# Attention with mixed heads and two MLPs: first two pulls on two queues, two score pairs behind the first mix, weight passes four steps behind each load

## The chip, the cores and the metric

The kernel runs on one core of one Trainium2 chip. The metric is the device time of one execution in microseconds (us), lower is better. The core has five engines with an instruction queue each: PE (matrix multiplies into PSUM), ACT, DVE and POOL (elementwise work), and SP, which here only issues DMA transfers. An engine executes its queue in order; a transfer that is issued runs beside the engines.

## What is computed

The reference, cut to what matters (`B, H, S, D = 2, 12, 448, 64`):

```python
scores = scale * (q @ k^T)                       # per batch and head, 448 x 448
scores = einsum('bhij,hg->bgij', scores, w_pre)  # mix over the 12 heads
attn   = softmax(scores, axis=-1)
attn   = einsum('bhij,hg->bgij', attn, w_post)   # mix over the heads again
x      = attn @ v                                # then (B*S, H*D) = (896, 768)
h      = x @ w_in;  x = (h * relu6(h + 3) / 6) @ w_out       # 768 -> 2048 -> 768
h      = x @ w_in2; x = (max(h,0) + alpha*min(h,0)) @ w_out2 # 768 -> 2048 -> 768
```

## The kernel before

**Tiles, groups, steps.** The 896 query rows are cut into 8 tiles of at most 120 rows (120, 120, 120, 88 per batch). The scores of a tile lie in SBUF as `S[row, head, key]`; three such buffers are used in turn. Six *score pairs* make one tile: a pair is the `q k^T` of two heads (`qk_parts`, line 205, PE), brought from PSUM to SBUF by one copy on ACT and one on DVE. For the mix over heads, ten rows of all 12 heads have to lie on 120 partitions; a *pull* (`pull`, line 221) is the DMA that moves one such group of rows there, SBUF to SBUF. There are 90 groups, and a *step* `p_` treats two of them, so there are 45 steps (`NP`). The pulls of step `p_ + 3` are issued in step `p_`, into four buffers that are used in turn.

**One step.** `premix` (line 234) multiplies the two pulled groups with `w_pre`, gives the row maxima (`nm`, line 242, DVE) and lets one score pair of a later tile run between its matmuls; `exp` (line 251, ACT) gives `e` and the row sums; `norm` (lines 258 to 263) scales `w_post` by the inverse sums into `wr` (on POOL up to step 36, on DVE from step 37, `late_from`); `post` (line 274, PE) of the step before multiplies `e` with `wr`; `post_evac` (line 289) copies the result to `MT`, two copies on ACT, from the end of the score pairs on one of them on DVE. `av` (lines 320 and 341, PE) multiplies finished tiles with `v`. The scheduler is off (`tc.manual_schedule()`): every engine's order is the order in which the loop `for p_ in range(-2, NP + 1)` writes its instructions.

**Score pairs.** The table `qk_at` says in which step a pair runs. Before step 0 there are two steps, -2 and -1, that hold only pairs of tile 1, three in each; from step 0 to step 35 there is one pair in each step. The loads of `q` (`load_q_at`) hang on this table.

**Loads on SP.** All pulls and nearly all loads are issued by SP, in the order of the code: first `q` and `k` of batch 0, `w_pre`, then the pulls of steps 0 to 2 with `w_post` between the fourth and the fifth. In steps 3 to 6 `v` of batch 0 is loaded, `q` of tiles 3 and 4 in steps 3 and 6, `k` of batch 1 in steps 7 to 12, one load a step, behind the pulls of that step.

**First weight blocks.** The MLP weights come as 64-bit words and are turned into a high and a low 32-bit part by passes: `conv_abs` (line 411) and `conv_low` (417) on ACT, `conv_shift` (427, 428) and `conv_sign` (435) on DVE, `conv_round` (442) on POOL, then `conv_hi` (447, ACT) and `lo_parts` (455, POOL). Blocks 0 to 2 are loaded during the attention, each in two halves, through one staging buffer (`early_wst`), so the load of a block follows `conv_round` of the one before. The table says in which step the load begins (17, 24, 31) and when the passes run: `conv_abs` and `conv_shift` in step 19, 27, 33, `conv_low` and `conv_sign` two steps later, `conv_round` three. `conv_hi` runs in steps 38, 42 and 44. From step 38 on, ACT and POOL also split `xT` into two parts (lines 524 and 525), and from step 42 the first matmuls of the MLP (line 529) run between the steps.

Of the kernel before, what the change touches and what calls it, by code (L numbers as in the profile page):

```python
# [17 lines left out]
Q = 64  # L18
# [17 lines left out]
def kernel(  # L36
# [15 lines left out]
    nc = tc.nc  # L52
    _, D, H, S = k.shape
# [10 lines left out]
    GH = G2 * H  # L64
# [44 lines left out]
    with tc.manual_schedule():  # L109
# [26 lines left out]
        def load_q(ti, *at, qs=(nc.sync, nc.sync)):  # L136
            T = tiles[ti]
            n = T["n"]
            m = H // 2 * n
            if ti == 2:  # L140
                t = late.tile([128, WC, 2], F32, tag="early_wst", bufs=1, name="qst")
                t = q_st[ti] = t.rearrange("p n o -> p (n o)")[:, :Z + H // 2 * GP]
            else:
                t = q_st[ti] = kq.tile([128, Z + H // 2 * GP], F32, tag="qst", bufs=2, name="qst")
            nc.gpsimd.memset(t[:, :Z], 0.0)
            z = Q + m - n + upper(n)
            if z > Z + m:
                nc.gpsimd.memset(t[:, Z + m:z], 0.0)
            at = (0, *at, H // 2)
            for x, y in zip(at, at[1:]):  # L150
                for o in range(2):
                    d = slice(D * o, D * o + D)
                    a = T["i0"] * H
                    if T["b"]:
                        a += o * m
                        nc.sync.dma_start(
                            out=t[d, Z + x * n:Z + y * n], in_=q[T["b"], d, a + x * n:a + y * n]
                        )
                        continue
                    src = q[T["b"], d, a:a + H * n].rearrange("p (j o n) -> p j o n", o=2, n=n)  # L160
                    qs[o].dma_start(
                        out=t[d, Z + x * n:Z + y * n].rearrange("p (j n) -> p j n", n=n),
                        in_=src[:, x:y, o, :],
                    )
                yield
# [194 lines left out]
        qk_at, av_at, av_first = {}, {}, {}  # L360
        marked = {NTILE - 1}
        for i in range((NTILE - 1) * (H // 2)):
            p_ = i // 3 - 2 if i < H // 2 else i - H // 2
            qk_at.setdefault(p_, []).append((1 + i // (H // 2), i % (H // 2)))
        for ti in range(NTILE - 1):
            lo = (tiles[ti]["s"] + tiles[ti]["ng"] - 1) // 2 + 2
# [243 lines left out]
        for c in range(2):  # L610
            a = GH * c
            nc.sync.dma_start(out=wpre[Z + GH * c:Z + GH * c + GH, :GH], in_=w_pre[a:a + GH, a:a + GH])
        list(load_q(2))
        for _ in range(4):
            d_buf.append(late.tile([128, 2, S], F32, tag=f"pull{len(d_buf)}", bufs=1, name="pull"))
            nc.gpsimd.memset(d_buf[-1][:Z], 0.0)
# [2 lines left out]
            v_c.append(late.tile(shape, F32, tag=f"v{c}", bufs=1, name=f"v{c}"))  # L619
        seen = late.tile([128, 16], F32, tag="rest", bufs=1, name="rest")[:, :1]  # L620
        nc.gpsimd.tensor_scalar(wpre, wpre, scale, 1.0, ALU.mult, ALU.mult)

        def s_out(pairs):
            for o, (d, s_) in enumerate(pairs):
# [9 lines left out]
            also.setdefault(s_, []).extend(fs)  # L634

        before_post = {}
        for i, a in enumerate((17, 24, 31)):
            odd = (a + 2) | 1
            for z in range(2):
                at(2 * (a + z), lambda z=z, i=i: load_w(i, z, 2))  # L640
            for s_, f in ((odd, conv_abs), (odd + 2, conv_low)):
                before_post.setdefault(s_, []).append(lambda f=f, i=i: f(i))
            for s_, f in ((odd, conv_shift), (odd + 2, conv_sign), (odd + 3, conv_round)):
                at(2 * s_, lambda f=f, i=i: f(i))
# [23 lines left out]
        load_at = {}  # L668
# [4 lines left out]
                load_at.setdefault(s_, []).append(lambda b=b, x=x: load_v(b, *x))  # L673

        for c in range(H // 2):
            load_at.setdefault(7 + c, []).append(
                lambda c=c: load_k(1, c % 2, c // 2 * 2, c // 2 * 2 + 2)
            )

        for p_ in range(-2, NP + 1):  # L680
            if p_ == -2:
                for g in range(6):
                    if g == 4:
                        for c in range(2):
                            a = GH * c
                            nc.sync.dma_start(
                                out=wraw[Q * c:Q * c + GH], in_=w_post[a:a + GH, a:a + GH]
                            )
                        nc.gpsimd.tensor_copy(
                            wpost.rearrange("p (g x) -> p x g", g=H),  # L690
                            wraw.rearrange("p (x g) -> p x g", g=H),
                        )
                    pull(g)
            late_pull = None
            if 0 <= p_ < NP - 3:
                g = 2 * p_ + 6
                pull(g)
                if groups[g][0] == groups[g + 1][0]:
                    pull(g + 1)
                else:  # L700
                    late_pull = g + 1
            for f in load_at.get(p_, []):
                f()
            for ti in load_q_at.get(p_, []):
                list(load_q(ti))
            jobs = qk_at.get(p_, [])
            pair_ = None
            if 0 <= p_ < NP:
                if jobs:
                    emit, pair_ = qk_parts(*jobs[0], "sc")  # L710
                    premix(p_, emit)
                    nc.scalar.copy(*pair_[1])
                    jobs = jobs[1:]
                else:
                    premix(p_)
            two = [lambda ti=ti, j=j: qk(ti, j, "mx" if p_ < 0 and j % 2 == 0 else "sc") for ti, j in jobs]
            pend = [f() for f in (two if p_ < 0 else [])]
            if 0 <= p_ < NP:
                exp(p_)
            for s_ in pend:  # L720
                s_out(s_)
            if pair_:
                nc.vector.tensor_copy(*pair_[0])
            if p_ >= 0:
                for f in two:
                    s_out(f())
            if late_pull:
                pull(late_pull)
            for ti, a in av_first.get(p_, []):
                av(ti, a)  # L730
            kk = 2 * (p_ - (NP - KD // 2))
            if kk == 0:
                p0 = ptile()[:, :S]
            if 0 <= kk < KD:
                in_part(p0, 0, x_t, 0, kk, kk + 2)
            for f in before_post.get(p_, []):
                f()
            if 1 <= p_:
                post(p_ - 1)
                post_evac(p_ - 1)  # L740
            if 0 <= p_ < NP:
                norm(p_)
            x1_split()
            if p_ == NP:
                p1 = ptile()[:, :S]
                in_part(p1, 1, x_t, 0, 0, 2)
                gs[0, 0] = g_tile(0, 0)
                run(act1(p0, gs[0, 0], 0))
            for f in also.get(2 * p_, []) + also.get(2 * p_ + 1, []):
                f()  # L750
            for ti, a in av_at.get(p_, []):
                av(ti, a)
# [153 lines left out]
```

## Time and profile before

| | us |
|---|---|
| median of 3 runs (641.83, 645.3, 645.5) | 645.3 |
| the profiled execution, whole | 640.25 |
| its span, from the first to the last instruction | 638.5 |
| PE busy in the span | 627.0 (98%) |
| DVE, ACT, POOL busy | 415.9, 345.3, 294.0 |

The attention fills about the first 180 us of the span, the two MLPs the rest. Rows of the profile give times in us from the start of the span. In the chain of work, each piece is what the end of the program was waiting for at that time, followed back from the last instruction. In a timeline, a bracket behind a row says how long the engine sat idle before it and what ended that.

### The profile page before, as it was taken

How to read it: one execution, taken by the hardware profiler on the slowest of the kernel's cores; microseconds unless marked ns; L12 is line 12 of the kernel's file. 1: busy time of each engine (PE TensorE's matmuls, PEld its weight loads, DVE VectorE, ACT ScalarE, POOL GpSimd, SP SyncE). 2: the span in 40 equal slices, each digit the busy share in tenths (PEclk: the TensorE clock that was granted, in tenths of full speed). 3: DMA queues.
4: the chain of work that ended last, by engine and by line, in shares of the span. 5: the costliest groups of instructions: out<-in, count | busy, mean ns of one | idle time of the engine just before them, and what ended most of it. 6: DMA issues, size and time to landing. Idle time of an engine off the chain costs nothing.

```text
span 638.5 us, 15698 instructions
## 1 busy us (share of the span) xinstructions
PE 627.0 (98%) x6528; PEld 537.2 (84%) x6528; DVE 415.9 (65%) x653; ACT 345.3 (54%) x632; POOL 294.0 (46%) x241
## 2 busy tenths in 40 slices
PE   7999999999999999999999999999999999999997
PEld 3466667666799999999999999999999999999997
DVE  3765677778666878787545533599999996544301
ACT  4886888987645566655345433444444444444301
POOL 2221123324615454556774645355555556776430
PEclk9999999999999999999999999999999999999999
DMA  7677765756012323333442333123333333445202
GB/s 187 222 197 211 207 188 204 214 177 174 34 50 100 99 100 107 125 115 101 148 148 100 112 136 100 51 100 99 100 102 110 113 113 108 149 159 180 94 1 86
DMA packets 42163, 81.69 MB, mean 128 GB/s; under 512 B 19308, under 2 KB 32364, under 8 KB 42092
## 3 DMA queue, kind: packets, MB, share of 16 engines
q1 hardware_dynamic: 41516, 80.27, 39.5%
q8 instruction: 51, 0.84, 0.5%
q10 hardware_dynamic: 576, 0.41, 0.3%
q14 instruction: 20, 0.16, 0.1%
HBM read 58.65 MB, written 2.75 MB: 96 GB/s over the span
## 4 chain that ended last, share of the span: by engine, by line
PE 86%; POOL 4%; issue 4%; DMA 3%; DVE 1%; ACT 1%; POOLq 0%; SPq 0%; ACTq 0%
PE p L529 64%; PE sc L205 6%; PE pt L274 5%; PE mx L234 5%; PE av L341 4%; POOL wb L442 2%; POOL wlo L455 2%; DMA wst<-in_w_in_dram 2%; PE av L320 1%; DMA pull<-S 1%; ACT e L251 0%; DMA qst<-in_q_dram 0%; ACT wb L411 0%; DVE wb L427 0%; DVE wb L428 0%
## 5 line engine op out<-in xcount | busy, mean ns | idle before, releaser
L455 POOL TENSOR_TENSOR wlo<-wb,whi 128x768 fp32r<-128x768 f32 (+1 forms) x67 | 128.5, 1918 | 122.4 <-ACT whi L447 122.4
L442 POOL TENSOR_TENSOR wb<-wb,wst 128x768 int32<-128x768 int32 x64 | 125.6, 1963 | 81.7 <-DVE wb L435 67.5
L529 PE MATMUL p<-xh,whi 128*128 128x448 f32 x384 | 140.0, 364 | 0.0
L529 PE MATMUL p<-xl,whi 128*128 128x448 f32 x384 | 139.4, 363 | 0.0
L529 PE MATMUL p<-gl,whi 128*128 128x448 f32 x384 | 139.3, 363 | 0.0
L529 PE MATMUL p<-gh,wlo 128*128 128x448 f32 x384 | 138.9, 362 | 0.2 <-POOL wlo L455 0.2
L529 PE MATMUL p<-gh,whi 128*128 128x448 f32 x384 | 138.8, 361 | 0.0
L529 PE MATMUL p<-xh,wlo 128*128 128x448 f32 x384 | 138.3, 360 | 0.0
L427 DVE TENSOR_SCALAR wb<-wb 128x768 f32<-128x768 f32 x64 | 52.6, 822 | 83.4 <-ACT wb L411 83.4
L411 ACT ACTIVATE wb<-wst 128x768 f32<-128x768 f32 x64 | 58.0, 906 | 72.9 <-DMA wst<-in_w_out_dram 51.8
L447 ACT CAST whi<-wb 128x768 fp32r<-128x768 f32 x64 | 53.4, 834 | 47.7 <-PE p L529 29.5
L529 PEld LDWEIGHTS p<-xh,whi 128*128 128x128 f32 x384 | 72.1, 188 | 8.0 <-issue 1.6
L205 PE MATMUL sc<-kst,qst 64*64 64x448 f32 (+2 forms) x384 | 74.7, 575 | 3.7 <-DMA qst<-in_q_dram 3.7
L234 PE MATMUL mx<-pull,wpre 64*64 64x448 f32 (+2 forms) x360 | 74.6, 544 | 2.6 <-ACT e L251 1.7
L529 PEld LDWEIGHTS p<-gh,whi 128*128 128x128 f32 x384 | 72.0, 187 | 5.2
L529 PEld LDWEIGHTS p<-gh,wlo 128*128 128x128 f32 x384 | 71.9, 187 | 5.1 <-POOL wlo L455 0.6
L529 PEld LDWEIGHTS p<-gl,whi 128*128 128x128 f32 x384 | 72.1, 188 | 4.8
L529 PEld LDWEIGHTS p<-xh,wlo 128*128 128x128 f32 x384 | 71.8, 187 | 5.0
L529 PEld LDWEIGHTS p<-xl,whi 128*128 128x128 f32 x384 | 72.1, 188 | 3.9
L242 DVE TENSOR_REDUCE nm<-mx 128x1 f32<-128x448 f32 x90 | 55.1, 622 | 20.2 <-PE sc L205 8.9
L435 DVE SCALAR_TENSOR_TENSOR wb<-wst,wb 128x768 uint32<-128x768 uint32 x64 | 67.5, 1054 | 1.1
L263 POOL TENSOR_SCALAR wr<-wpost,sm 128x60 f32<-128x60 f32 x74 | 24.4, 345 | 93.8 <-DVE sm L259 46.6
(55 smaller groups left out, 772.7 us busy)
## 6 DMA issues: line engine op xcount, KB each, us to landing
wst<-in_w_out_dram SPq DMA_DIRECT2D x32, 768.0 KB
wst<-in_w_in_dram SPq DMA_DIRECT2D x27, 768.0 KB
pull<-S SPq DMA_DIRECT2D x88, 210.0 KB
wst<-in_w_in_dram SPq DMA_DIRECT2D x10, 384.0 KB
out_dram<-o SPq DMA_DIRECT2D x12, 224.0 KB
kst<-in_k_dram SPq DMA_DIRECT2D x11, 224.0 KB
qst<-in_q_dram SPq DMA_DIRECT2D x10, 180.0 KB
v<-in_v_dram SPq DMA_DIRECT2D x4, 168.0 KB
```

The source lines that it names most:

```text
L205: nc.tensor.matmul(ps[o][r:r + z - a, :S], t[D * o:D * o + D, a:z], k_[D * o:D * o + D, j, :], start=True, stop=True,)
L234: nc.tensor.matmul(ms[r][Q * c:Q * c + Q, :S], wpre[a:z], d[a:z, c, :], start=True, stop=True)
L242: nc.vector.tensor_reduce(nm, m[:, :S], axis=AX.X, op=ALU.max, negate=True)
L274: nc.tensor.matmul(ts[c][Q * z:Q * z + Q, u:u + GH], e[a:a + GH, j:j + Q], wr[a:a + GH], start=True, stop=True,)
L341: nc.tensor.matmul(by_half(p[D * o:D * o + D, a % 3, :2 * m]), v_part(T["b"], h, t), MT[ti][:, t:2 * NJ:NJ, h, :m].rearrange("p r (o x) -> ...
L411: nc.scalar.activation(t, s[:, :, 1].bitcast(F32), ACTF.Abs)
L427: nc.vector.tensor_scalar(t, t, W_MAX, W_MIN, ALU.min, ALU.max)
L435: nc.vector.scalar_tensor_tensor(u, st_t[i][:, :, 1], 0xC0000000, u, ALU.bitwise_and, ALU.bitwise_or)
L442: nc.gpsimd.tensor_tensor(n, n, st_t.pop(i)[:, :, 0].bitcast(I32), ALU.add)
L447: nc.scalar.copy(hi, b_t[i])
L455: nc.gpsimd.tensor_tensor(lo[:, a], b_t[i][:, a], w_t[i][0].bitcast(F32)[:, a], ALU.subtract)
L529: nc.tensor.matmul(p, wt[a], xt[c], start=(first and z == 0), stop=(last and z == 2))
```

## The change

Three things. First, `w_post` is loaded and laid out before any pull, and the pull of group 1 is issued by ACT's queue while SP issues the others. Second, `qk_at` is moved: two pairs each in steps -2 and -1, two in step 0 behind its mix and its `exp`, then one in each of steps 1 to 36; the loads of `q` from tile 3 on and of `k` of batch 1 move by one step with it. Third, the blocks are loaded from steps 17, 25, 33, and the passes run four steps behind: `conv_abs` and `conv_shift` in 21, 29, 37, `conv_low` and `conv_sign` in 23, 31, 39, `conv_round` in 24, 32, 40.

```diff
         for i in range((NTILE - 1) * (H // 2)):
-            p_ = i // 3 - 2 if i < H // 2 else i - H // 2
+            p_ = i // 2 - 2 if i < 4 else max(i - 5, 0)
             qk_at.setdefault(p_, []).append((1 + i // (H // 2), i % (H // 2)))
...
         list(load_q(2))
+        for c in range(2):
+            a = GH * c
+            nc.sync.dma_start(out=wraw[Q * c:Q * c + GH], in_=w_post[a:a + GH, a:a + GH])
...
         nc.gpsimd.tensor_scalar(wpre, wpre, scale, 1.0, ALU.mult, ALU.mult)
+        nc.gpsimd.tensor_copy(
+            wpost.rearrange("p (g x) -> p x g", g=H), wraw.rearrange("p (x g) -> p x g", g=H)
+        )
...
-        for i, a in enumerate((17, 24, 31)):
-            odd = (a + 2) | 1
+        for i, a in enumerate((17, 25, 33)):
+            odd = a + 4
...
-            load_at.setdefault(7 + c, []).append(
+            load_at.setdefault(8 + c, []).append(
                 lambda c=c: load_k(1, c % 2, c // 2 * 2, c // 2 * 2 + 2)
             )
...
             if p_ == -2:
                 for g in range(6):
-                    if g == 4:
-                        for c in range(2):
-                            a = GH * c
-                            nc.sync.dma_start(
-                                out=wraw[Q * c:Q * c + GH], in_=w_post[a:a + GH, a:a + GH]
-                            )
-                        nc.gpsimd.tensor_copy(
-                            wpost.rearrange("p (g x) -> p x g", g=H),
-                            wraw.rearrange("p (x g) -> p x g", g=H),
-                        )
-                    pull(g)
+                    pull(g, nc.scalar if g == 1 else nc.sync)
...
-                if jobs:
+                if jobs and p_:
                     emit, pair_ = qk_parts(*jobs[0], "sc")
                     premix(p_, emit)
```

Three places show what moves. On PE, around the first mix (`sc` is a score pair's PSUM tile, `mx` the mix's, `qst_115` is `q` of tile 1, `qst_121` of tile 2), before:

```order
L205 MATMUL sc_235<-kst_91,qst_115 64x448
L205 MATMUL sc_235<-kst_91,qst_115 60x448
L234 MATMUL mx_251<-pull_125,wpre_95 64x448 x2
L205 MATMUL sc_250<-kst_91,qst_121 64x448
L205 MATMUL sc_250<-kst_91,qst_121 60x448
L234 MATMUL mx_252<-pull_125,wpre_95 64x448 x2
L205 MATMUL sc_249<-kst_91,qst_121 64x448
L205 MATMUL sc_249<-kst_91,qst_121 60x448
L234 MATMUL mx_282<-pull_127,wpre_95 64x448 x2
```

and now:

```order
L205 MATMUL sc_221<-kst_91,qst_115 60x448
L234 MATMUL mx_232<-pull_127,wpre_95 64x448 x2
L234 MATMUL mx_233<-pull_127,wpre_95 64x448 x2
L205 MATMUL sc_247<-kst_91,qst_115 64x448
L205 MATMUL sc_247<-kst_91,qst_115 60x448
L205 MATMUL sc_248<-kst_91,qst_115 64x448
L205 MATMUL sc_248<-kst_91,qst_115 60x448
L205 MATMUL sc_255<-kst_91,qst_115 64x448
L205 MATMUL sc_255<-kst_91,qst_115 60x448
L205 MATMUL sc_256<-kst_91,qst_115 64x448
L205 MATMUL sc_256<-kst_91,qst_115 60x448
L234 MATMUL mx_274<-pull_129,wpre_95 64x448 x2
```

The first mix (`mx_232`, `mx_233`) stands in one piece ahead of the last two pairs of tile 1, and these stand ahead of the second mix; tile 2 begins one step later.

On SP, steps 6 to 8 (`v_134` and, renumbered, `v_136` are the same tile), before:

```order
L221 DMA pull<-S 120x1x448 x2
L177 DMA v_134<-in_v_dram 96x6x64
L177 DMA v_134<-in_v_dram 32x6x64
L177 DMA v_134<-in_v_dram 80x6x64
L177 DMA v_134<-in_v_dram 48x6x64
L156 DMA qst<-in_q_dram 64x720 x2
L221 DMA pull<-S 120x1x448 x2
L119 DMA kst<-in_k_dram 64x896
```

and now:

```order
L221 DMA pull<-S 120x1x448 x2
L177 DMA v_136<-in_v_dram 96x6x64
L177 DMA v_136<-in_v_dram 32x6x64
L177 DMA v_136<-in_v_dram 80x6x64
L177 DMA v_136<-in_v_dram 48x6x64
L221 DMA pull<-S 120x1x448 x2
L156 DMA qst<-in_q_dram 64x720 x2
L221 DMA pull<-S 120x1x448 x2
L119 DMA kst<-in_k_dram 64x896
```

The pulls of step 7 (used in step 10) now stand ahead of `q` of tile 4, and the pulls of step 8 ahead of the first load of `k`.

On DVE, from step 37 to the maxima of step 38, before:

```order
L289 COPY MT<-pt 128x84x5
L258 TENSOR_SCALAR sm<-sm 128x2
L259 RECIPROCAL sm<-sm 128x2
L263 TENSOR_SCALAR wr<-wpost,sm 128x60 x2
L242 TENSOR_REDUCE nm<-mx 128x1 x2
```

and now:

```order
L289 COPY MT<-pt 128x84x5
L258 TENSOR_SCALAR sm<-sm 128x2
L259 RECIPROCAL sm<-sm 128x2
L263 TENSOR_SCALAR wr<-wpost,sm 128x60 x2
L427 TENSOR_SCALAR wb<-wb 128x768
L428 TENSOR_SCALAR wb<-wb 128x768
L242 TENSOR_REDUCE nm<-mx 128x1 x2
```

The two `conv_shift` passes of block 2, which stood ahead of the maxima of step 34, now stand ahead of those of step 38; in the same way its `conv_sign` moves from ahead of step 36 to ahead of step 40.

## Rows read from the trace of the kernel before

**Rows 1.** The page, part 4: shares of the span in the chain, by engine.

```profile
PE 86%; POOL 4%; issue 4%; DMA 3%; DVE 1%; ACT 1%; POOLq 0%; SPq 0%; ACTq 0%
```

**Rows 2.** Chain in order of time (start us, length us, what), 40 to 240 us.

```profile
43.11 4.75 DMA pull<-S
47.99 1.50 PE mx L234 x3
...
50.65 0.87 PE pt L274 x49
...
94.18 0.59 PE mx L234 x2
...
95.92 1.38 PE av L341 x24
...
132.29 0.56 DVE wb L428
...
138.38 0.76 PE mx L234 x8
...
148.40 0.81 PE pt L274 x48
...
180.56 59.60 PE p L529 x297
```

**Rows 3.** Timeline of all engines (start us, length us, what), 12 to 20 us.

```profile
12.56 3.42 SPq L221 DMA_DIRECT2D pull<-S  x4
...
16.34 0.59 PE L234 MATMUL mx<-pull,wpre 64*64 64x448 f32 x2
...
18.56 0.64 ACT L251 ACTIVATE e<-mx,nm 128x448 f32<-128x448 f32 x1
...
19.34 0.59 PE L234 MATMUL mx<-pull,wpre 64*64 64x448 f32 x2 [0.51 <-ACT e L251]
```

**Rows 4.** Timeline of SP, 41 to 46 us.

```profile
41.83 1.19 SPq L156 DMA_DIRECT2D qst<-in_q_dram  x2
43.11 1.78 SPq L221 DMA_DIRECT2D pull<-S  x2
44.95 0.75 SPq L119 DMA_DIRECT2D kst<-in_k_dram  x1
```

**Rows 5.** Windows: start:end length, busy by engine, clock, DMA share, GB/s.

```profile
40.00:50.00 10.00, 8.67 (x205) 5.68 (x200) 4.74 (x12) 6.36 (x17) 1.20 (x4) 1.00 0.72 204
50.00:60.00 10.00, 10.00 (x238) 6.83 (x234) 6.70 (x16) 8.30 (x21) 1.21 (x4) 1.00 0.80 216
```

**Rows 6.** Timeline of ACT, 83 to 134 us.

```profile
83.83 0.92 ACT L411 ACTIVATE wb<-wst 128x768 f32<-128x768 f32 x1 [1.39 <-DMA wst<-in_w_in_dram]
...
86.57 0.63 ACT L251 ACTIVATE e<-mx,nm 128x448 f32<-128x448 f32 x1 [0.50 <-DVE nm L242]
...
110.16 0.91 ACT L411 ACTIVATE wb<-wst 128x768 f32<-128x768 f32 x1
...
130.66 0.92 ACT L411 ACTIVATE wb<-wst 128x768 f32<-128x768 f32 x1 [0.91 <-DMA wst<-in_w_in_dram]
...
133.48 0.63 ACT L251 ACTIVATE e<-mx,nm 128x448 f32<-128x448 f32 x1 [0.56 <-DVE nm L242]
```

**Rows 7.** Timeline of DVE, 138 to 155 us.

```profile
138.14 0.96 DVE L435 SCALAR_TENSOR_TENSOR wb<-wst,wb 128x768 uint32<-128x768 uint32 x1
...
144.81 0.41 DVE L263 TENSOR_SCALAR wr<-wpost,sm 128x60 f32<-128x60 f32 x2
...
152.78 0.60 DVE L289 COPY MT<-pt 128x420 f32<-128x420 f32 x1 [0.78 <-PE pt L274]
...
153.69 1.35 DVE L263 TENSOR_SCALAR wr<-wpost,sm 128x60 f32<-128x60 f32 x2
```

**Rows 8.** Timeline of POOL, 142 to 155 us.

```profile
142.62 1.86 POOL L442 TENSOR_TENSOR wb<-wb,wst 128x768 int32<-128x768 int32 x1
...
153.85 1.14 POOL L525 TENSOR_TENSOR xl<-xT,xh 128x448 fp32r<-128x448 f32 x1 [0.66 <-ACT xh L524]
```

## The prediction

> **What bounds the kernel now.** I read the shares of the chain first: PE holds 86% of the span [rows 1]. The chain in order of time says where: from 180.56 on it is MLP matmuls without a break for as far as I read it [rows 2], so what the attention wins or loses by then, the whole program wins or loses, and the MLP itself gives nothing. None of the edits takes work away, so only gaps in the attention's 180 us can be won. Those that the edits touch are four. At the start the second mix waits 0.51 for an `exp` [rows 3]. At 43.11 a pull stands in the chain for 4.75 us [rows 2]. And twice ACT waits for a weight block: 1.39 us before the `conv_abs` at 83.83 and 0.91 before the one at 130.66, each with a second wait for DVE behind it (0.50, 0.56); the middle block at 110.16 waits for nothing [rows 6]. Durations are those of the profiled execution, 640.25 us for a span of 638.5; the median of the runs shown is 645.3, 5 us above it, and their spread (641.83 to 645.5) is as large as all that follows. I make the sum as a difference and apply it to the median.
>
> **Start: 0 (-0.9 to +0.8).** Before, the first mix runs at 16.34 behind six pairs, its `exp` at 18.56, the second mix at 19.34 [rows 3]. Four pulls take SP 3.42 us, 0.86 each [rows 3], so a second queue brings the second pull up to 0.86 forward, and with two pairs fewer ahead of it the mix may begin that much sooner. But the gain meets a queue. The two pairs now stand behind the mix on PE and share one pair of PSUM buffers; ACT copies the first only after both halves of `exp` 0, so the second pair waits for that copy, and the second mix stands behind it on PE. `norm` 0 on DVE likewise stands behind two copies. The price of ACT's own issue is not shown for a pull; from SP's row it is 0.86, spent while it has four pairs still to copy. I take 0: the early mix buys nothing for the second one. Ends: a whole pull's issue won, or the time of one pair's copies, about one exposed `exp` pass and issue (0.64 + 0.2), lost. `w_post` before the pulls costs nothing; SP waits there for the scores anyway.
>
> The Trainium skill speaks against the two queues: "DMA: Bandwidth & Descriptors", section "Issuing engines are not separate DMA queues", says that transfers issued by different engines run on the same 16 DMA engines and only the issuing time is saved. By that rule this term can be no more than the one issue, which is the end I have; no row here shows where the two pulls would collide.
>
> **One more step with a pair: +0.9 (0 to +1.0).** Two pairs leave the stretch before the first mix, and step 36, which had none, gets one. A mix with its pair takes PE 1.74 us (94.18 to 95.92), without one 0.76 [rows 2]; the difference is 0.98. PE is the chain there, so I take nearly all of it; nothing, if PE would have waited for DVE in that step.
>
> **Pulls ahead of `q` and `k`: -1.3 (-2.7 to 0).** In step 10 the pull ends at 47.86 (43.11 + 4.75), and the mix with its pair lasts from 47.99 to 50.65, 2.66 us against 1.74: it is still waiting in the middle, for the second pull [rows 2]. SP issued `q` of tile 4 at 41.83, right ahead of these pulls at 43.11 [rows 4]; now they go first, 1.28 us sooner. The pulls of step 8 lose the `k` load ahead of them, 0.75 of issue [rows 4]. But the DMA moves 204 and 216 GB/s here at a share of 0.72 and 0.80 [rows 5], so I reckon with a backlog: a load put behind is paid for by the next pulls. What stays won at the end of the stretch is one `k` load, 64 x 896 x 4 B = 229 KB, 1.1 us at 204 GB/s. Between 1.28 and 1.1 with a little more from the `w_post` loads: -1.3. Upper end: the whole of the late mix (0.92) and its wait in full with those of the steps behind, -2.7 as an estimate; nothing, if the next mixes are late by the same.
>
> **Block 0: -1.4 (-1.9 to -0.5).** Its load keeps its step and `conv_abs` goes from step 19 to 21, about two steps later; the load had landed 1.39 into the wait, so the wait goes. The 0.50 behind it is DVE's passes standing ahead of the row maxima; it comes back in step 22, so I leave it out. The round now ends one step ahead of the next block's load, which SP must hold for it, with the pulls of step 26 behind it. They are for step 29; three steps cover it. Without that cover one round, 1.86 [rows 8], is late. Block 1 had no wait and keeps its distance: 0.
>
> **Block 2, where it was: -1.4 (-1.5 to 0).** Load from 31 to 33, `conv_abs` from 33 to 37. The 0.91 goes, and since the passes leave this place, nearly all of the 0.56 as well [rows 6].
>
> **Block 2, where it comes to: +1.5 (0 to +3.0).** Steps 37 to 40 are those in which DVE, no longer POOL, makes `wr` as well. Two `conv_shift` passes (0.56 the one [rows 2], the other taken as equal, 1.12) now stand between `wr` 37 and the maxima of step 38, and `conv_sign`, 0.96 [rows 7], ahead of those of step 40. Behind the maxima wait `exp`, `norm` and `post`; `post` at 148.40 is in the chain [rows 2]. That is 2.08 us of DVE. The widest hole behind them is the 0.78 before 152.78 [rows 7]; against it, 1.3 is exposed. Besides, `wr` takes 0.41 alone and 1.35 with POOL's split of `xT` beside it (153.85, 1.14) [rows 7, 8]; POOL's round, 1.86 [rows 8], now runs in step 40, ahead of that split, so one more `wr` may be caught: 0 to 0.94. I take 0.2 of that, together 1.5. Ends: holes take all, or 2.08 + 0.94.
>
> On this the Trainium skill is harsher: "SBUF — State Buffer", section "Who interferes with whom", says that DVE in its two-port modes and a GpSimd instruction exclude each other for a whole instruction. The 1.35 beside the 1.14 agrees with it. By that rule a `wr` that meets the start of the round would stand for all of 1.86, this term would be 1.3 + 1.86 = 3.2 and the sum 0.0; that is most of the way to the second rival below, whose price is made from rows.
>
> **Sum:** 0 + 0.9 - 1.3 - 1.4 - 1.4 + 1.5 = **-1.7 us**: 638.6 for the profiled execution, **643.6** for the median.
>
> **Rivals.**
> *The holes hold (20%).* Steps 37 to 40 hide the passes and step 36 the pair. For it: DVE has a hole of 0.78 left [rows 7], and the span's DVE is far from full. Against it: `wr` is on DVE's path there. Then -1.3 - 1.4 - 1.4 = -4.1: 641.2.
> *DVE becomes the bound at the end (17%), slower.* In steps 37 to 41 every microsecond put ahead of the row maxima comes out behind `post`, and the round catches `wr` twice: 2.08 + 2 x 0.94 = 4.0, with the pair of step 36 4.9. The gains in front are at most 1.3 + 1.4 + 1.4 = 4.1, so it ends at +0.8: 646.1. It decides from 3.2 us of DVE and POOL delay on (4.1 - 0.9). For it: the 1.35 [rows 7]. Against it: the passes may meet PE's own long steps.
> *The order of the loads does nothing (13%).* The stretch from 40 to 60 us is bound by transfer, not by order: pulls that go first make later ones late, and the new first step eats 0.3. Then -1.4 - 1.4 + 0.9 + 1.5 + 0.3 = -0.1: 645.2. For it: 216 GB/s in the second window [rows 5]; against it: the mix at 47.99 waited for pulls behind a load that is used six steps later.
>
> **How the numbers follow.** The forecast has 50%, about 642.3 to 645.1 by itself. The terms' ends, added, reach from 638 to beyond 648, but they will not all fall on one side: I take -4.5 to +1.5. The runs before lie up to 3.5 below their median, so the low end goes lower than the sum asks, and half a us for runs goes on top: 639.0 to 647.3. One per cent is 6.45 us, about what a measurement here can tell from no change. Faster by more needs every gain whole and a fast median: 6%. Slower by more needs the slower rival twice over: 3%. Within: 91%.
>
> **What would show it.** Right: no DMA wait before any of the three early `conv_abs`; the chain's pull piece at 43 gone or under 2 us; the second mix within 0.8 us of 19.34; `exp` of step 36 to that of step 37 longer by 0.9; DVE without gaps from step 37 to 40 and `post` there waiting for `wr`. Wrong: the second mix well before 18.5 (the start does give something), steps 37 to 41 no longer than before (the holes held), or a pull in the chain at a later place for as long as before. If the MLP's stretch changes its length, the ground of all this is wrong.

## The result: slower by 0.8%, and the profile after

The changed kernel takes **648.54 us** (median of 14 runs, 645.78 to 653.11), the kernel before 644.41 beside it (14 runs, 639.63 to 649.04): ratio 1.008, 95% interval 1.0051 to 1.011, that is 3.3 to 7.1 us slower. The ratio is taken over the single runs without those in a slower state, so it is not the quotient of the medians (1.0064). The prediction said 1.7 us faster and at most 647.3. The change stays within 1%, but the sign is wrong and the time lies outside the range.

The profiled execution of the changed kernel took 645.78 us, the lowest of its 14, with a span of 644.0, 5.5 more than before; the profile of before (640.25) is near the lowest of its runs too. The chain's shares, against [rows 1], show where to look:

```profile
PE 84%; POOL 4%; issue 4%; ACT 2%; DVE 2%; DMA 1%; SPq 1%; ACTq 0%; POOLq 0%; DVEq 0%
```

PE and DMA give shares up, ACT, DVE and SP gain them. Where that happens is told best by the time from one step's first `exp` to that of a later step (ACT, line 251, read off the timelines; us):

| stretch, by the starts of `exp` | before | after | block 2 alone | start alone | order alone |
|---|---|---|---|---|---|
| 0 to 2 | 5.40 | 7.77 | 5.79 | 7.77 | 5.38 |
| 2 to 7 | 13.01 | 14.65 | 13.38 | 13.47 | 13.54 |
| 7 to 9 | 7.46 | 7.42 | 6.72 | 6.80 | 7.42 |
| 9 to 13 | 16.58 | 13.43 | 17.88 | 15.66 | 13.72 |
| 13 to 20 | 25.56 | 26.07 | 26.63 | 25.61 | 25.27 |
| 20 to 27 | 22.26 | 22.49 | 22.26 | 24.01 | 22.21 |
| 27 to 34 | 24.65 | 24.14 | 23.71 | 24.70 | 26.38 |
| 34 to 37 | 9.02 | 9.70 | 9.01 | 9.70 | 10.66 |
| 37 to 44 | 24.50 | 28.98 | 28.71 | 24.64 | 24.49 |
| `exp` of step 44 at | 167.00 | 172.54 | 172.28 | 171.12 | 167.56 |

The last three columns are experiments, told below. `exp` 44 comes 5.54 us later than before, as much as the whole span grew, so the MLP behind it kept its length, as the prediction's ground wants. Three stretches lose over 1 us (0 to 2, 2 to 7, 37 to 44), one gains (9 to 13). The column of block 2 alone shows how far single executions differ: up to step 30 that kernel does the same as the one before, and yet 9 to 13 and 13 to 20 take 1.3 and 1.1 us longer.

**The start.** Timeline of the changed kernel, 12 to 23 us, against [rows 3]:

```profile
12.26 1.66 ACTq L221 DMA_DIRECT2D pull<-S  x1
...
16.20 1.10 PE L234 MATMUL mx<-pull,wpre 64*64 64x448 f32 x8
...
17.88 0.63 ACT L251 ACTIVATE e<-mx,nm 128x448 f32<-128x448 f32 x1 [1.02 <-DVE nm L242]
...
19.69 0.98 PE L205 MATMUL sc<-kst,qst 64*64 64x448 f32 x8 [1.64 <-ACT S L631]
...
20.49 0.92 PE L234 MATMUL mx<-pull,wpre 64*64 64x448 f32 x4
...
22.74 0.64 ACT L251 ACTIVATE e<-mx,nm 128x448 f32<-128x448 f32 x1
```

The first `exp` is 0.68 earlier (17.88 against 18.56). Then the second of the two pairs waits 1.64 for ACT's copy, which stands behind both halves of `exp` 0, and the second mix stands behind that pair: 20.49 against 19.34 before. `exp` 2 begins at 25.64 instead of 23.95, and the second mix, which was to stay within 0.8 of 19.34, misses that sign by 0.35.

**`q` of tile 3.** Timeline of SP and, below, the chain:

```profile
30.90 3.12 SPq L177 DMA_DIRECT2D v<-in_v_dram  x4
34.13 1.36 SPq L161 DMA_DIRECT2D qst<-in_q_dram  x2
```

```profile
34.84 3.90 DMA qst<-in_q_dram
...
38.88 1.08 PE sc L205 x8
```

It now stands in step 4, behind four loads of `v`, and lands where its first pair wants it; PE waits 1.1 us for it and steps 7 and 8 (to `exp` 7 and 8) are 2.05 us longer than their 6.79 before. Before, it was loaded in step 3, ahead of them. This profile is a mild one. Six of the runs below have the same order there. PE waited 0.85 and 1.18 us in two of them; in the other four it waited 1.70 to 2.42, its granted clock then fell to the lower of its two levels (0.50, which is 1.2 instead of 2.4 GHz), and steps 7 and 8 took 11.2 to 12.9 us. In one of the four (the run without DVE's passes; timeline, and window with the columns of [rows 5]):

```profile
40.01 1.86 PE L205 MATMUL sc<-kst,qst 64*64 64x448 f32 x8 [2.28 <-DMA qst<-in_q_dram]
```

```profile
40.00:45.00 5.00, 4.99 (x30) 2.73 (x32) 1.15 (x2) 1.88 (x5) 0.00 (x0) 0.50 0.69 190
```

**The blocks.** ACT's `conv_abs` of the three blocks waits for nothing now, against [rows 6]:

```profile
91.10 0.91 ACT L411 ACTIVATE wb<-wst 128x768 f32<-128x768 f32 x1
...
117.51 0.91 ACT L411 ACTIVATE wb<-wst 128x768 f32<-128x768 f32 x1
...
144.79 0.91 ACT L411 ACTIVATE wb<-wst 128x768 f32<-128x768 f32 x1
```

Step 20 (from `exp` 19 to `exp` 20) falls from 5.51 to 4.56, step 34 from 5.16 to 4.23.

**The end.** DVE and, below it, POOL and ACT of the changed kernel, 146 to 160 us, against [rows 7] and [rows 8]:

```profile
146.26 0.55 DVE L427 TENSOR_SCALAR wb<-wb 128x768 f32<-128x768 f32 x1
146.84 0.56 DVE L428 TENSOR_SCALAR wb<-wb 128x768 uint32<-128x768 uint32 x1
...
153.02 0.95 DVE L435 SCALAR_TENSOR_TENSOR wb<-wst,wb 128x768 uint32<-128x768 uint32 x1
...
156.44 2.66 DVE L263 TENSOR_SCALAR wr<-wpost,sm 128x60 f32<-128x60 f32 x2
```

```profile
156.14 1.81 POOL L442 TENSOR_TENSOR wb<-wb,wst 128x768 int32<-128x768 int32 x1
157.93 1.12 POOL L525 TENSOR_TENSOR xl<-xT,xh 128x448 fp32r<-128x448 f32 x1
...
148.03 0.63 ACT L251 ACTIVATE e<-mx,nm 128x448 f32<-128x448 f32 x1 [1.84 <-DVE nm L242]
...
159.73 0.64 ACT L251 ACTIVATE e<-mx,nm 128x448 f32<-128x448 f32 x1 [2.92 <-DVE nm L242]
```

`exp` 38 waits 1.84 (1.39 before) for maxima behind the two shift passes. In step 40 `wr` begins 0.30 behind POOL's round and takes 2.66 until 159.10. The row is two instructions: the first takes 1.57 and ends 0.05 behind the round (157.95), the second takes 1.17 and ends 0.05 behind the split that follows the round (159.05). `exp` 41 waits 2.92 (1.89 before). The windows there (columns as in [rows 5]) show a second price:

```profile
156.00:158.20 2.20, 0.26 (x10) 0.07 (x5) 2.13 (x4) 0.81 (x2) 2.20 (x3) 1.00 0.80 188
158.20:159.90 1.70, 1.38 (x56) 1.25 (x59) 1.70 (x3) 0.17 (x1) 0.85 (x1) 0.73 0.85 283
159.90:162.00 2.10, 2.10 (x21) 0.70 (x14) 2.03 (x8) 2.09 (x6) 0.00 (x0) 0.50 0.87 334
```

While `wr` is held, PE works 0.26 of 2.20 us; in the third window its granted clock is 0.50, with PE busy all the time. Step 43, behind it, takes 5.38 instead of 3.91.

### The profile page after: what moved, and what is told of

Read it like the earlier page. It is cut to its first block, busy times and chain, and to the rows that moved or that the text cites. A ratio compares the mean times of both kernels' runs of the same rounds, so it can differ in the third digit from the quotient of the medians.

```text
span 644.0 us, 15691 instructions
## 1 busy us (share of the span) xinstructions
PE 626.7 (97%) x6528; PEld 537.8 (84%) x6528; DVE 415.5 (65%) x652; ACT 345.2 (54%) x633; POOL 293.8 (46%) x241
## 4 chain that ended last, share of the span: by engine, by line
PE 84%; POOL 4%; issue 4%; ACT 2%; DVE 2%; DMA 1%; SPq 1%; ACTq 0%; POOLq 0%; DVEq 0%
PE p L529 64%; PE sc L205 5%; PE pt L274 5%; PE av L341 4%; PE mx L234 4%; POOL wb L442 2%; POOL wlo L455 2%; ACT e L251 1%; PE av L320 1%; DMA qst<-in_q_dram 1%; DVE nm L242 1%; ACT MT L289 1%; DVE wr L263 1%; SPq L177 0%; ACTq L221 0%
```

## The experiments

The theory at first: the loss is the slower rival's at the end, the two pairs at the start, and `q` of tile 3; the gains in front are real. The rivals to it stand in each expectation.

### 1. Block 2 back ahead of step 37, the rest as changed

```diff
-        for i, a in enumerate((17, 25, 33)):
-            odd = a + 4
+        for i, a in enumerate((17, 24, 31)):
+            odd = (21, 27, 33)[i]
```

> The changed kernel with blocks 1 and 2 as before (loads in steps 24 and 31, passes from 27 and 33); block 0 keeps its new distance. Theory A (the passes of block 2 load DVE in steps 37 to 41, where it already makes wr): exp 37 to exp 43 goes back from 24.4 us to about 20.5 (19.9 before, plus the pair of step 36), the wait of about 0.9 for block 2's load in step 34 returns, and the whole is 3 to 4 us below the changed kernel, ratio to before about 1.001. Rival B (the pair in step 36 and the order of the late steps are the cost): the stretch stays above 23 us and the whole changes by less than 1 us.

Measured: 651.32 us, ratio 1.0121 (1.0062 to 1.018) to the kernel before, so slower still. The end did what was expected: 37 to 44 took 24.27. But step 28 took 6.63 and step 34 8.73. With block 0's passes two steps later and block 1's load in the step where it was before, SP held that load for block 0's round, and step 28 waited for it; in step 34 block 2's load was late too. The chain and the windows (columns as in [rows 5]) there:

```profile
136.16 4.45 DMA wst<-in_w_in_dram
```

```profile
140.00:145.00 5.00, 2.78 (x64) 2.22 (x68) 2.86 (x6) 3.83 (x9) 0.00 (x0) 0.62 0.66 250
145.00:150.00 5.00, 5.00 (x100) 2.97 (x95) 2.73 (x9) 3.36 (x8) 0.60 (x2) 0.69 0.15 59
```

`conv_abs` waited 4.59 for block 2's second half; PE, idle for nearly half of the first window, had a granted clock of 0.69 in the second with full work. Loads and passes of successive blocks hang together through the one staging buffer: this undoes one part and breaks another.

### 2. The start: one queue, three pairs ahead, `q` of tile 3 ahead of `v`

Three single edits to the changed kernel:

```diff
-                    pull(g, nc.scalar if g == 1 else nc.sync)
+                    pull(g)
```

> The changed kernel with the pull of group 1 on SP again. In the changed kernel ACT was held 1.66 us by that issue. Theory A (the first mix waits for the pulls, and the second mix for the pairs behind exp 0, so ACT's issue costs little): first mix at 16.2 to 16.4, exp 1 at 22.4 to 22.9, as in the changed kernel (22.74). Rival B (ACT's issue is the cost at the start): exp 1 about 1.5 us earlier, near 21.2, as before (21.25).

```diff
-            p_ = i // 2 - 2 if i < 4 else max(i - 5, 0)
+            p_ = i // 3 - 2 if i < H // 2 else i - 5
```

> The changed kernel with all six pairs of tile 1 ahead of the first mix again, three in each of steps -2 and -1, none in step 0; all else as changed. Theory A (the two pairs behind exp 0 are the cost at the start): exp 0 later than 17.88, near 18.8, but exp 1 earlier, 21.2 to 21.9 instead of 22.74. Rival B (ACT's own issue of a pull is the cost): exp 1 stays at 22.7 or goes to 23 and more, since the copies of two more pairs now stand behind that issue.

```diff
-                    load_q_at.setdefault(p_ - (6 if ti == tps else 3), []).append(ti)
+                    load_q_at.setdefault(p_ - (6 if ti == tps else 4 if ti == 3 else 3), []).append(ti)
```

> The changed kernel with q of tile 3 loaded in step 3 as before, ahead of the four v loads of step 4; all else as changed. Theory A (q of tile 3 came late because it fell behind those v loads): the chain's piece of 3.90 us on that load goes, step 7 takes 2.6 instead of 4.29 us; part of it comes back in steps 9 to 11, where pulls are the limit, so exp 13 is 0 to 1 us earlier than 61.15. Rival B (the stretch is bound by transfer in any case): exp 13 does not move, and step 10 is longer by what step 7 wins.

Measured, one execution each: 649.5, 648.58 and 647.1 us; single times differ by several us from run to run, so the steps decide. With one queue `exp` 1 began at 22.73 (22.74 with two): ACT's pull, 1.66 us of issue instead of SP's 0.86 [rows 3], neither costs nor gains. With three pairs ahead `exp` 0 began at 19.30, but `exp` 1 at 21.78, which is 0.96 earlier; the change had made it 1.49 later. So the two pairs behind `exp` 0 are most of the cost. With `q` of tile 3 back in step 3, step 7 took 2.90 instead of 4.29, and 1 to 13 took 37.27 instead of 38.41: that load's place cost 1.1 us in the mild profile, and 2.8 to 4.9 against the four whose clock fell (40.11 to 42.20).

### 3. Each part alone on the kernel before

Block 2 alone:

```diff
-        for i, a in enumerate((17, 24, 31)):
-            odd = (a + 2) | 1
+        for i, a in enumerate((17, 24, 33)):
+            odd = (19, 27, 37)[i]
```

> The kernel before with one part of the change alone: block 2 loaded from step 33, its passes in steps 37 to 40. Theory A (the slower rival of the prediction: in steps 37 to 43 every microsecond of DVE's passes, and of POOL's round beside wr, comes out behind post): the stretch from exp 37 to exp 44, 24.5 us in the kernel before and 29.0 in the changed one, becomes 28 to 29.3; step 34, 5.16 in the kernel before, becomes 4.2; together +2.8 to +4.0 us, ratio 1.004 to 1.006. Theory B (the forecast's term of +1.5, most of it hidden, and something else of the change made the end longer): the stretch is 25.5 to 26.5, the whole +0.1 to +1.1 us. Theory C (the end is longer because the score pairs moved by a step): the stretch stays at 24.5 and the whole is 0.9 us shorter.

Measured: ratio 1.0027 (1.0001 to 1.0054). Step 34 fell to 4.23 and 37 to 44 took 28.71: theory A in the steps, +4.2 against -0.9. The ratio lies between A and B; its interval holds A's lower end and all of B's, so the steps decide for A and the time does not. C is out.

Start and order of loads without the blocks (the changed kernel with the table of blocks of before, so the lines of the diff above turned back):

> The changed kernel with the table of the weight blocks of before (loads from 17, 24, 31, passes in 19, 27, 33), so the new start and the new order of loads alone. Theory A: the stretch from exp 37 to exp 44 is back at 24.5 (from 29.0), the waits before the passes of blocks 0 and 2 are back (steps 20 and 34 at 5.5 and 5.2 us), the start keeps its +1.7 by step 2, steps 7 and 8 their +2.0 for q of tile 3, steps 9 to 13 their -3.6, step 37 the pair's +0.7: together +0.8 us against the kernel before, up to +2.1 if step 15 stalls again as it did in the changed kernel; ratio 1.001 to 1.003. Theory B (start and order of loads are what made the kernel slower): the ratio stays at 1.006 to 1.010.

Measured: ratio 1.0051 (1.0022 to 1.0081), between A's numbers and B's, with an interval that overlaps both; 37 to 44 is back at 24.92. So not all of the loss is at the end. With block 2 alone it makes 1.0051 x 1.0027 = 1.0078, the whole, which leaves nothing for the later passes of block 0. Step 20 took 4.28 here, though block 0 stands where it was.

The order of loads alone:

```diff
-                    load_q_at.setdefault(p_ - (6 if ti == tps else 3), []).append(ti)
+                    load_q_at.setdefault(p_ - (5 if ti == tps else 3), []).append(ti)
...
-            load_at.setdefault(7 + c, []).append(
+            load_at.setdefault(8 + c, []).append(
```

> The kernel before with only the order of loads of the change: q of tile 4 in step 7 and the loads of k in steps 8 to 13, so each behind the pulls of one more step; start, score pairs and q of tile 3 as before. Theory A (the term of -1.3 holds): the pull leaves the chain at 43, exp 7 to exp 13 falls from 24.05 to 21.9 to 22.8 us, ratio 0.997 to 0.999. Theory B (the third rival: that stretch is bound by transfer, not by order): exp 7 to exp 20 stays within 0.5 us of 49.6, ratio 0.999 to 1.002.

Measured: 643.12 us against 643.2, ratio 0.9999 (0.9969 to 1.0028), which is B's number but does not shut out A's. In its profile, against B, the pull is gone from the chain and 9 to 13 falls from 16.58 to 13.72, but step 34 takes 6.87, since `conv_abs` of block 2 waits longer than before, and then PE runs at a lower clock (timeline of ACT; window with the columns of [rows 5]):

```profile
129.71 0.89 ACT L411 ACTIVATE wb<-wst 128x768 f32<-128x768 f32 x1 [2.73 <-DMA wst<-in_w_in_dram]
```

```profile
134.00:138.00 4.00, 4.00 (x48) 1.96 (x44) 1.98 (x6) 2.78 (x8) 0.60 (x2) 0.65 0.05 19
```

The start alone (the changed kernel with the blocks of before, `k` from step 7 and `q` one step sooner, in the steps where they were):

```diff
-                    load_q_at.setdefault(p_ - (6 if ti == tps else 3), []).append(ti)
+                    load_q_at.setdefault(p_ - (7 if ti == tps else 4), []).append(ti)
...
-            load_at.setdefault(8 + c, []).append(
+            load_at.setdefault(7 + c, []).append(
```

> The kernel before with only the start of the change: w_post ahead of the pulls, the second pull on ACT's queue, two pairs behind exp 0 and one pair more in step 36; the loads of q and k in the steps in which they were, the weight blocks as before. Theory A (the two pairs in step 0 are lost time, and nothing later takes it back): exp 2 at 25.6 us instead of 23.95, step 37 at 3.3 instead of 2.6, so +2.4 us, ratio 1.0025 to 1.0045. Theory B (the steps from 7 on wait for transfers anyway, so a later start is taken back there): exp 2 at 25.6, but exp 13 within 0.5 us of 61.0; only the pair of step 37 stays, ratio 1.000 to 1.0015.

Measured: ratio 1.0073 (1.0039 to 1.0106), 2.5 to 6.8 us: by whole times the dearest part of all, above A's number with an interval that holds A's upper end. Theory A's steps are there (0 to 2 takes 7.77, step 37 3.29). `exp` 0 came at 18.75 in this profile, so `exp` 2 is at 26.51, 2.56 later than before; with the pair that is 3.2. By `exp` 13 it is 1.44, so some of it is taken back, as B says, but not kept: step 27 holds a pause in the middle of a `post` for which the chain names nothing but PE's own issue:

```profile
108.36 1.53 issue
109.89 0.50 PE pt L274 x18
```

### 4. What the passes and the round cost at the end

The changed kernel without POOL's round of block 2, then without DVE's three passes of block 2:

```diff
-                at(2 * s_, lambda f=f, i=i: f(i))
+                if (i, f) != (2, conv_round):
+                    at(2 * s_, lambda f=f, i=i: f(i))
```

> The changed kernel without POOL's conv_round of block 2 (the 32-bit add of step 40 is left out, so the high and low parts of block 2 are unrounded). Theory A (POOL's round holds DVE off for its whole length): the wr of 2.66 us beside it is 1.35 or less, and the stretch from exp 37 to exp 44 falls from 29.0 to 27.2 to 27.9 us. Theory B (the 2.66 comes from the split of xT beside it): one wr of over 2 us is still there and the stretch stays within 0.5 us of 29.0.

```diff
+                if (i, f) not in ((2, conv_shift), (2, conv_sign)):
```

> The changed kernel without DVE's passes of block 2 (conv_shift and conv_sign are left out, so block 2 is split wrongly). Theory A (every microsecond ahead of the row maxima comes out behind post): the stretch from exp 37 to exp 44 falls from 29.0 by the 2.06 us of the three passes, to 26.5 to 27.3. Theory B (holes on DVE hide half or more of them, and the round is what costs): it falls by less than 1.0 us.

Measured: without the round 37 to 44 takes 25.57, 3.4 less, twice theory A's; without the passes 27.63, 1.35 less, between A and B. The first fence is DVE without the round, the second DVE and POOL without the passes:

```profile
160.67 0.41 DVE L263 TENSOR_SCALAR wr<-wpost,sm 128x60 f32<-128x60 f32 x2
```

```profile
163.77 2.66 DVE L263 TENSOR_SCALAR wr<-wpost,sm 128x60 f32<-128x60 f32 x2
...
163.47 1.81 POOL L442 TENSOR_TENSOR wb<-wb,wst 128x768 int32<-128x768 int32 x1
```

Take the round away and `wr` in step 40 is 0.41; keep it and it is 2.66, whatever else DVE does. Without the round the stretch saves more than the 2.25 of the one `wr`, because the lower clock behind it is gone too (step 43 4.24 instead of 5.38). Without the passes steps 38 and 40 are 1.76 shorter, nearly the 2.06 that the passes take, as A says; what is missing went to step 41, which took 0.74 more with a clock that fell earlier in it.

### 5. Earlier loads instead of later passes

```diff
-        for i, a in enumerate((17, 24, 31)):
-            odd = (a + 2) | 1
+        for i, a in enumerate((16, 23, 30)):
+            odd = a + 3
```

> The kernel before, with the blocks loaded from steps 16, 23, 30 and the passes three steps behind (19, 26, 33), all else as it was: instead of later passes, earlier loads. Theory A (the waits before the passes of blocks 0 and 2 are lateness of the load alone, and the passes cost nothing where they stood): step 20 falls from 5.52 to 4.2 to 4.6 us, step 34 from 5.16 to 4.2 to 4.6, exp 37 to exp 44 stays at 24.5; -1.5 to -2.3 us, ratio 0.9965 to 0.998. Theory B (what a wait gives back is lost elsewhere, since the loads now compete with other transfers): the steps shorten but steps 15 to 18 or 27 to 33 grow by as much; ratio 0.999 to 1.002.

Measured: 640.92 us, ratio **0.9967** (0.9938 to 0.9996). Step 20 falls to 4.18, step 34 to 4.73 (a wait of 0.51 is left), and 37 to 44 stays at 24.28. The interval nearly touches 1, and step 20 alone proves little: with block 0 untouched it took 4.21 to 4.28 in three of the runs above (block 2 alone, blocks undone, start alone), where no wait for its load was left either, and 5.31 with the order alone.

The same with the order of loads of the changed kernel:

> The kernel before with the blocks loaded a step earlier (16, 23, 30, passes three steps behind) and with q of tile 4 and the loads of k one step later, behind the pulls. In the run with the order of loads alone exp 20 came 2.75 us earlier than in the kernel before, but step 34 lasted 6.87 (for block 2's load) and steps 35 and 36 at a lower clock took 1.6 more, and the median was the same. Theory A (the order's gain is real and was given back at block 2's wait): with that wait gone most of both gains stay, -3 to -5 us, ratio 0.992 to 0.996. Theory B (the stretch from 40 to 80 us is bound by transfer and its length varies from run to run; the order gives nothing): the same as with the earlier loads alone, ratio 0.9955 to 0.998.

Measured: 641.84 us, ratio 0.996 (0.9928 to 0.9991): theory B, no more than the earlier loads alone. The pulls of step 7 now go ahead of `q` of tile 4 (first fence, SP) and land in time. But those of step 8, at 45.81, stand behind it, and the second of them is in the chain (second fence) for longer than the one in [rows 2]; step 11's mix waits 0.82 for it. Against [rows 2] the wait stands one step further on. That is not shown to come from the order: with the old order and the same earlier loads a pull of step 8 is in the chain too (third fence), issued at nearly the same time:

```profile
42.45 1.69 SPq L221 DMA_DIRECT2D pull<-S  x2
44.23 1.47 SPq L156 DMA_DIRECT2D qst<-in_q_dram  x2
45.81 1.76 SPq L221 DMA_DIRECT2D pull<-S  x2
```

```profile
46.75 5.21 DMA pull<-S
```

```profile
46.78 5.23 DMA pull<-S
```

With block 2's passes four steps behind the load, but packed into steps 34 to 36:

```diff
-            odd = a + 3
+            odd = a + 3 + i // 2
...
+            t = odd + 2 - i // 2
```

(`t` is the step of `conv_low` and `conv_sign`, `t + 1` that of the round.)

> The same, with block 2's passes four steps behind its load but still ahead of step 37: conv_abs and conv_shift in step 34, conv_low and conv_sign in 35, conv_round in 36. Theory A (a wait of 0.5 us is left before conv_abs of block 2 in step 33 with the load in step 30): step 34 falls from 4.7 to 4.2, another -0.5 us against the kernel with three steps. Theory B (conv_sign right behind conv_shift stands ahead of maxima in a row and costs as much): no difference, within 0.1 per cent of it.

Measured: 643.1 us, ratio 0.999 (0.9957 to 1.0024), no better. Step 34 falls to 4.23 (5.44 in the run before this one), but steps 35 to 37 take 10.13 instead of 9.02: theory B. Its profile also has the longest pause of PE on record for which the chain names nothing else, again inside a `post`:

```profile
71.08 3.47 issue
74.55 0.36 PE pt L274 x3
```

The changed kernel with the start of before, and with it `q` of tile 3 in step 3:

> The changed kernel with the start of before (three score pairs each in steps -2 and -1, one pair in step 0 and none in step 36, all pulls on SP, w_post between the fourth and the fifth; q of tile 3 in step 3), so the later passes and the order of loads alone. Theory A (the start costs 2.4 us by the steps that it lengthens, and what was measured beyond that, 4.7 with the start alone, is scatter of the stretches behind it): 2.0 to 3.0 us under the changed kernel, ratio to the kernel before 1.003 to 1.005. Theory B (the later start costs near 5 us, since it moves all that follows against the transfers): ratio 1.000 to 1.002.

Measured: 645.06 us, ratio 1.003 (0.9996 to 1.0064): 0.5% or 3.2 us under the changed kernel (1.008), a little above A's 2.0 to 3.0, with a ratio at A's lower end; the interval is too wide to shut B out, and the 3.2 holds the place of `q` of tile 3 as well. In this profile too a pull of step 8 holds the chain, for 5.31 us.

## Why the prediction was wrong, step by step

**Block 2, where it comes to: +1.5. In the steps this term failed most; it measured +4.5** (24.50 to 28.98), and +3.0 to +4.6 in the six profiles with the passes and the round there (27.47 to 29.06), against an upper end of 3.0. What failed is the overlap. I subtracted a hole of 0.78 on DVE, but that hole is DVE waiting for `post` [rows 7], which stands behind the same maxima: it hid nothing, and the passes came out nearly whole (step 38 lost 1.12 for 1.11 us of passes, step 40 0.87 for 0.95). Step 41 lost 1.03, for which I had taken 0.2: `wr` met the round whole, 2.66 instead of 1.35. Step 43 lost 1.47 to the lower clock, which was in no term and came in three of the six. The mechanism was that of the slower rival (17%), whose chance was far too low. That its 4.0 is near the 4.5 is in part luck: the round caught `wr` in one step, not in two, and the clock made up for it. The rule that I set beside it (the Trainium skill, "SBUF — State Buffer", section "Who interferes with whom") gave 3.2 for this term, and the trace agrees with it: each of the two instructions of the 2.66 ends 0.05 behind one of POOL's, and without the round they take 0.41.

**Start: 0 (-0.9 to +0.8). It measured +1.7 in the steps to `exp` 2, and by the time of the run with it alone, the pair of step 36 included, this part missed by most** (2.5 to 6.8 us, forecast 0.9). ACT's copy does stand behind both halves of `exp` 0, as I wrote, but I priced that as one exposed pass. The pairs wait for each other through the one pair of PSUM buffers, and all of it stands ahead of the second mix: PE waited 1.64 for the copy and had one pair more, 0.98, to do. What they left empty ahead of the first mix brought it only 0.68, since PE waits there anyway (1.15 us for a copy, ahead of the last pair). The rule on issuing engines ("DMA: Bandwidth & Descriptors" of the Trainium skill, section "Issuing engines are not separate DMA queues") says that only issuing time can be saved, and the run agrees: one queue instead of two moved `exp` 1 by 0.01.

**The pair of step 36: +0.9.** Right: 3.29 instead of 2.61, +0.7.

**Pulls ahead of `q` and `k`: -1.3.** Not borne out, though not shut out either: 0.9999 alone, an interval of -2.0 to +1.8 us, and nothing seen on top of the earlier loads. 9 to 13 took 13.7 to 14.1 in three of the five profiles with the new order and `q` of tile 3 in its place, 17.3 and 17.7 in the other two, and 15.7 to 20.5 in the four with the old order; in the run with the order alone, what the stretch won was lost again by step 37. The third rival (13%) names the outcome, but its reason, that pulls which go first make later ones late, is not shown: a pull of step 8 was late with either order (5.21 and 5.31 us in the chain with the new, 5.23 with the old). And a move of the same edit was in no term: `q` of tile 3 slid behind four `v` loads, though following every load of a moved step would have found it. It is 2.05 in steps 7 and 8 of the changed kernel's profile, 1.1 by the run that turned it back, and more where the clock fell behind the wait. The order shown ahead of the prediction began at step 6, behind the place.

**Block 0: -1.4, and block 2 where it was: -1.4.** Both inside their ranges, -0.95 and -0.93, in this pair of profiles; of the wait for DVE, 0.34 is left before `exp` 20. But the waits that they remove are not steady. Block 0's was gone in three runs without any change to block 0, and block 2's, 0.91 before, was 2.73 with the order alone and absent with the start alone. So block 0's gain is not shown to be the change's.

**The sum.** With terms measured in the one profile: 1.7 + 0.7 + (2.05 - 3.61 for steps 7 to 13) - 0.95 - 0.93 + 4.48 = +3.4, of +5.5 in the profile; 1.3 more is step 15, where PE's `post` starts late, with 0.54 of issue in the chain, and the rest is small. In the median it is 648.54 - 644.41 = +4.1.

**What the runs settle, and what stays open.** The start costs 3.2 us by the steps of the run with it alone, 4.7 by that run's ratio. The clock of the runs accounts for most of the difference, as far as so few runs can tell: its four runs with a mean granted clock of 0.999 or more took 644.7 us in the mean, the 17 such runs of the kernel before beside it 641.7, so 3.0 more; but 8 of its 12 runs lay lower, against 12 of 29. Undoing the start gave 3.2 too, with `q` of tile 3 in it.

The stretch from step 9 on differs between profiles with the same order of loads there (9 to 13: 15.66 with the start alone, 16.58 before, 17.88 with block 2 alone, 20.45 with the earlier loads). Part of such differences are the pauses of PE for which the chain names nothing but issue (1.53 and 3.47 above). All that the traces show of them points to one cause: PE waits for its instructions. The page counts 51 transfers on one instruction queue, of 16 KB each, among the loads on the 16 DMA engines. Between 20 and 180 us, the chains of the 16 profiles hold 14 such pauses of 0.7 us or more. Each ends 1.3 to 1.7 us after one of these transfers ended, and if PE's matmuls, weight loads and semaphore instructions are counted in the trace, all 14 end at a count of 192 beyond a multiple of 256. What made those transfers late was not tried.

## What to carry to other kernels

When a pass waits for a load, move the load ahead before you move the pass back: the one gave 0.3% (interval 0.04% to 0.6%), the other cost more in the new place than the wait had. Before work goes to another step, list what is unique to the engines there (here `wr` on DVE and a round on POOL that keep each other waiting), and price a collision with the whole of the longer instruction and with the slower clock of PE behind it. And work ahead of the first result, where PE waits anyway, was cheap here (0.68 us for two pairs); behind it, it was paid in full. After a change of steps, list every load that moves with them, and what it now stands behind.

## What the runs showed of the hardware

Six profiles have block 2's passes and round in the steps of DVE's `wr`, all with the same held `wr` (2.66 or 2.67). In three of them PE's clock fell behind it (step 43 at 5.18 to 5.49), in three it did not (3.90 and 3.91): the same idle time is sometimes followed by some 3 us at 0.50, and the 1.47 lost there was more than what the held `wr` itself cost against before (1.03). That clock also separates the runs of one kernel. Of the 92 runs of the kernel before beside the experiments, the 45 with a mean granted clock of 0.999 or 1.0 took 641.8 us in the mean, the 36 at 0.996 and 0.997 took 644.3, the 11 below took 647.8. A pull issued by ACT beside one of SP's held ACT's queue for 1.42 to 1.67 us in eight profiles; one by SP alone takes 0.86.
